# Attention's outputs as eight 64-row products a tile, and k and v in tiles of 256 rows

## The chip, the cores and the metric

The kernel runs on one core of one Trainium2 chip. The metric is the device time of one execution in microseconds. A profile of one execution stands beside three timed ones. TensorE is called PE here (PEld is its weight loads), VectorE DVE, ScalarE ACT, GpSimd POOL and SyncE SP, as in the profile.

## The reference, cut to what matters

Three parts follow each other. Linear attention over 4 batches, 8 heads, 576 positions and heads of 64 is normalised head by head; its 2304 rows of 512 go through a mixture of 8 experts, one expert a row, and then through a dense feed-forward block:

```python
kv = np.einsum('bhsd,bhse->bhde', k, v)
out = np.einsum('bhsd,bhde->bhse', q, kv)
rms = np.sqrt(np.mean(out * out, axis=-1, keepdims=True) + 1e-06)
x = (out / rms * g_norm)
...
logits = x @ w_gate
expert_idx = np.argmax(logits, axis=1)
h = np.maximum(np.einsum('ecd,edf->ecf', disp, w1), 0.0)
y = np.einsum('ecf,efd->ecd', h, w2)
...
h = x @ w_in
g = np.where(h > 0.0, h, alpha * (np.exp(np.minimum(h, 0.0)) - 1.0))
return (g @ w_out)
```

`disp` holds each expert's rows in their order of arrival, up to a capacity.

## The kernel before, in words

**Attention** (lines 107 to 397) has its order written out by hand: inside it the instructions of each engine run as the program lists them. k and v come as [2304, 512], 18 chunks of 128 rows, q transposed as `qT` [4, 128, 2304]: partition = two heads of 64 features, four such pairs. `load_kv` (line 127) and `load_q` (line 132) issue all transfers on SP's queue, in the order of lines 267 to 289; the outputs' stores to `x_dram` go to the same queue behind them. The pool `ld` holds ten chunks of each.

Chunk by chunk `kv_product` (line 149) sums k'v of each head, 64 x 64, for one batch in PSUM (`pk`): head h of a pair goes to the column half h of PE. A batch is four chunks and a half. `kv_out`, `kv_turn` and `kv_gate` (lines 167 to 186) take the sums out, transpose them and multiply by `gw`, the gate's weights times `g_norm`, so that `kva` holds for each pair of heads k'v beside k'v·gw. `kva` is a 128 x 144 block for each pair, with zeros where a row belongs to one head and the column to the other; POOL clears it (line 141), and `yT` as well (line 144).

`out_tile` (line 195) makes the outputs of 128 tokens: for each of four pairs one product of 128 rows (both heads' features), 128 columns (tokens) and 144 moving columns. A tile that lies over the border of two batches (tiles 4 and 13) is made in two parts of 64 tokens. From PSUM (`po`, two buffers) ACT takes the squares and a copy (`oz_all`); for the tiles in `POOL_SQ` POOL squares the copy instead. `out_sums` (DVE) sums the squares of a head. `chain` is the routing of a group of tiles, split into steps that the program deals out between the tiles; its last group needs all 18. `fill` issues products that nobody reads: they keep PE busy. Lines 297 to 397 are the hand-written order.

**Routing** (lines 403 to 494) turns the choices into `ids`, the list of rows by expert. POOL then gathers rows from `x_dram` by these lists (`gather`, line 535).

**The first window** (`first_window`, line 616) prepares the first expert's 352 rows: three gathered tiles are scaled (DVE), transposed (PE), copied as high part `xh` (ACT) and low part `xl` (DVE). `h_piece` issues the first layer's products for the expert's first two slices u = 0 and 1 as rows become ready, 12 products for each slice and each piece of rows. Then come the 64 steps of the experts (`step`, line 973), where `place` scales and transposes further gathered rows, and the dense block.

Of the kernel before, what the change touches and what calls it, by code (L numbers as in the profile page):

```python
# [20 lines left out]
P = 128  # L21
# [20 lines left out]
def block_kernel(ctx, tc, qT, k, v, g_norm, w_gate, w1, w2, w_in, w_out, out, cap, **_):  # L42
# [27 lines left out]
    ld = early.enter_context(tc.tile_pool(name="ld", bufs=10))  # L70
# [4 lines left out]

    ones = const.tile([P, P], F16, name="ones")
# [30 lines left out]
    KA = D * 2 + 2 * E  # L107
    with ExitStack() as actx:
# [18 lines left out]
        def load_kv(c):  # L127
            for t, src, n in ((kt, k, "kt"), (vt, v, "vt")):
                t[c] = ld.tile([P, C], F32, name=n)
                nc.sync.dma_start(out=t[c], in_=src[c * P:(c + 1) * P])  # L130
# [8 lines left out]
        for b in range(B):  # L139
            t = ap1.tile([P, NP, KA], F32, name=f"kva{b}")  # L140
# [4 lines left out]
        HALF = [slice(0, D), slice(D, P)]  # L145

        pk = {}
# [23 lines left out]
        def kv_turn(b):  # L171

            pt = ps_t.tile([P, NP // 2, P], F32, name="pt")
            for n in range(NP // 2):
                nc.tensor.transpose(pt[:, n], kvs[b][:, n * P:(n + 1) * P], ident)
            for h in range(2):
                nc.scalar.activation(kva[b][HALF[h], :, h * D:(h + 1) * D], pk[b][HALF[h]], AF.Copy)
            kvT[b] = ap2.tile([P, NP // 2, P], F32, name="kvT")
            nc.vector.tensor_copy(kvT[b], pt)

        def kv_gate(b):
# [3 lines left out]
            for h in range(2):  # L185
                nc.vector.tensor_copy(kva[b][HALF[h], :, P + h * E:P + (h + 1) * E], pz[HALF[h], :, :, h].rearrange("p n a e -> p (n a) e"))

# [3 lines left out]
        oz_all = ap1.tile([P, NT, NP, KA], F32, name="oz_all")  # L191
# [3 lines left out]
        def out_tile(i):  # L195
            po = ps_o.tile([P, NP, 256], F32, name="po")
# [9 lines left out]
            o = oz[:, :, 0:P]  # L206
            if i in POOL_SQ:
                nc.scalar.activation(oz, po[:, :, 0:KA], AF.Copy)
                nc.gpsimd.tensor_tensor(out=sq, in0=o, in1=o, op=ALU.mult)
            else:  # L210
                nc.scalar.activation(sq, po[:, :, 0:P], AF.Square)
                nc.scalar.activation(oz, po[:, :, 0:KA], AF.Copy)
# [13 lines left out]
        def chain(i0, G):  # L226

            def t_(shape, name):
# [16 lines left out]
                                  in0=oz_all[:, i0:i0 + G].rearrange("p g j c -> p (g j) c")[:, :, P:KA].rearrange("p k (h e) -> p k h e", h=2),  # L245
# [21 lines left out]
        for c in range(3):  # L267
            load_kv(c)
        for h in range(2):
            nc.scalar.dma_start(out=g_col[HALF[h]], in_=g_norm.rearrange("(d o) -> d o", o=1))  # L270
        for a in range(2):
            for n in range(NP // 2):
                j = 2 * n + a
                nc.scalar.dma_start(out=wg[HALF[a], n], in_=w_gate[j * P:(j + 1) * P].rearrange("(h c) e -> c h e", h=2))
# [3 lines left out]
        for c in range(3, 5):  # L278
            load_kv(c)
        load_q(0, [(0, 256), (256, S)])  # L280
        for c in range(5, 9):
            load_kv(c)
        load_q(1, [(0, 320), (320, S)])
        for c in range(9, 14):
            load_kv(c)
        load_q(2, [(0, 256), (256, S)])
        for c in range(14, 18):
            load_kv(c)
# [9 lines left out]
        fill(6)  # L298
        for c in range(5):
            chunk(0, c, (3, 3, 4, 3, 0)[c])  # L300
# [9 lines left out]
        kv_product(1, 1, 2)  # L310
        out_tile(2)
        out_sums(1)
        kv_product(1, 2, 4)
        out_sums(2)
        kv_product(1, 4, 5)
        kv_out(1)
        out_tile(3)
        kv_turn(1)
        out_sums(3)
        step(ca, 1)  # L320
        fill(2)
        kv_gate(1)
        step(ca, 1)
        fill(2)
        out_tile(4)
        step(ca, 3)
        kv_product(2, 0, 1)
        out_tile(5)
        out_sums(4)
        step(ca, 2)  # L330
        kv_product(2, 1, 3)
        out_tile(6)
        out_sums(5)
        step(ca, 2)
        kv_product(2, 3, 5)
        kv_out(2)
        out_tile(7)
        kv_turn(2)
        out_sums(6)
        step(ca, 1)  # L340
        out_tile(8)
        kv_gate(2)
        out_sums(7)
        step(ca, 2)
        kv_product(3, 0, 3)
        step(ca, 4)
        out_tile(9)
        out_sums(8)
        step(cb, 1)
        kv_product(3, 3, 5)  # L350
        kv_out(3)
        step(cb, 1)
        out_tile(10)
        kv_turn(3)
        out_sums(9)
        step(cb, 3)
        out_tile(11)
        kv_gate(3)
        out_sums(10)
        step(cb, 2)  # L360
        out_tile(12)
        out_sums(11)
        step(cc, 1)
        step(cb, 3)
        out_tile(13)
        step(cc, 1)
        out_sums(12)
        step(cb, 2)
        step(cc, 2)
        out_tile(14)  # L370
        step(cb, 1)
# [4 lines left out]
        step(cc, 3)  # L376
        out_tile(16)
        out_sums(15)
        out_tile(17)
# [169 lines left out]
    def place_scale(a):  # L549
        xg = xg_t[a]  # L550
        v = xg[:, 0:C].rearrange("p (h d) -> p h d", h=H)
        nc.vector.scalar_tensor_tensor(out=v, in0=v, scalar=used[:, a:a + 1], in1=xg[:, C:C + H].to_broadcast([P, H, D]),
                                       op0=ALU.mult, op1=ALU.mult)
# [50 lines left out]
    def h_piece(u, w, low):  # L604
# [5 lines left out]
        for j in range(NP):  # L610
# [5 lines left out]
    def first_window(fill):  # L616
# [9 lines left out]
        def turn(a):  # L626
# [697 lines left out]
```

## Time and profile before

| | us |
|---|---|
| median of three timed executions (691.22 to 691.6) | 691.48 |
| the profiled execution | 690.72 |
| its span, first to last instruction | 688.9 |
| PE busy in the span | 674.6 (98%) |
| DVE, ACT, POOL busy | 478.8, 389.0, 101.8 |

The profiled execution has 1.8 us around its span and lies 0.76 us under the median. Times of rows are counted from the start of the span. The timeline merges neighbouring instructions of a line into one row, with the number of them behind an x; a product of 32-bit numbers counts as two instructions.

### The profile page before, as it was taken

Reading aid. Unit: us, or ns where it says so; the run is one execution under the profiler, and the core shown is the slowest. Engines: PE = TensorE matmul, PEld = TensorE weight load, DVE = VectorE, ACT = ScalarE, POOL = GpSimd, SP = SyncE. Lnnn points to the kernel's source line nnn. Section 1 sums busy time; section 2 is a strip of 40 time slices with the busy share of each in tenths; the row PEclk is TensorE's granted clock in tenths of the full one; section 3 lists DMA queues with packets and bytes.
Section 4 is the critical chain, followed back from the end, with each engine's and each line's share of the span. In section 5 each row is a group of like instructions: output and inputs, shape, how many; then the busy total and the mean of one; then the engine's idle time right before and its main releaser. Section 6 shows DMA issues by size and latency. Waiting matters only on the chain.

```text
span 688.9 us, 12042 instructions
## 1 busy us (share of the span) xinstructions
PE 674.6 (98%) x4282; PEld 630.3 (91%) x4282; DVE 478.8 (70%) x915; ACT 389.0 (56%) x821; POOL 101.8 (15%) x118
## 2 busy tenths in 40 slices
PE   8999899999999999999999999999999999999996
PEld 8888899999999999999999998888899999898995
DVE  5479476777777878978765457768767687765542
ACT  1474266555555666758766567555655657554450
POOL 7112483000001212005400000000000000002213
PEclk9999899999999999999999999999999999999999
DMA  8997774646556778945643819475374937357412
GB/s 276 394 321 198 233 218 155 206 131 217 173 185 186 234 256 273 289 147 189 227 152 117 356 47 368 152 289 204 148 283 160 361 105 298 111 210 279 178 48 91
DMA packets 67101, 145.82 MB, mean 212 GB/s; under 512 B 9312, under 2 KB 29280, under 8 KB 67040
## 3 DMA queue, kind: packets, MB, share of 16 engines
q1 hardware_dynamic: 63424, 135.44, 56.3%
q0 software_dynamic: 2880, 9.59, 4.0%
q8 instruction: 34, 0.56, 0.3%
q14 instruction: 27, 0.22, 0.1%
q10 hardware_dynamic: 736, 0.02, 0.1%
HBM read 118.92 MB, written 26.10 MB: 211 GB/s over the span
## 4 chain that ended last, share of the span: by engine, by line
PE 64%; issue 3%; POOL 1%; POOLq 0%
PE pa L1133 11%; PE acc L1174 6%; PE acc L1175 6%; PE acc L1173 6%; PE pd L1133 5%; PE ph L677 4%; PE ph L678 4%; PE ph L679 4%; PE pe L1133 3%; PE acc L1087 2%; PE acc L1088 2%; PE acc L1086 2%; PE acc L679 2%; PE acc L677 2%; PE acc L678 2%
## 5 line engine op out<-in xcount | busy, mean ns | idle before, releaser
L1133 PE MATMUL pa<-right,ab 128*128 128x384 f32 x432 | 84.5, 336 | 0.0
L1133 PEld LDWEIGHTS pa<-right,ab 128*128 128x128 f32 x432 | 76.2, 188 | 2.1 <-ACT u L1230 0.5
L677 PE MATMUL acc<-hh,w2h 128*128 128x288 f32 (+6 forms) x256 | 77.3, 302 | 0.0
L678 PE MATMUL acc<-hh,w2l 128*128 128x288 f32 (+6 forms) x256 | 76.9, 300 | 0.0
L679 PE MATMUL acc<-hl,w2h 128*128 128x288 f32 (+6 forms) x256 | 76.9, 300 | 0.0
L677 PE MATMUL ph<-xh,w1h 128*128 128x288 f32 (+6 forms) x248 | 75.0, 302 | 0.3 <-PEq L868 0.3
L678 PE MATMUL ph<-xh,w1l 128*128 128x288 f32 (+6 forms) x248 | 74.6, 301 | 0.0
L679 PE MATMUL ph<-xl,w1h 128*128 128x288 f32 (+6 forms) x248 | 74.4, 300 | 0.0
L1175 PE MATMUL acc<-w2h,gx 128*128 128x512 f32 x180 | 70.3, 390 | 0.0
L1174 PE MATMUL acc<-w2l,gx 128*128 128x512 f32 x180 | 70.2, 390 | 0.0
L1173 PE MATMUL acc<-w2h,gx 128*128 128x512 f32 x180 | 70.0, 389 | 0.0
L1181 POOL DMA_INDIRECT out<-part,ids x18 | 17.6, 977 | 324.3 <-DVE part L1178 314.7
L697 ACT ACTIVATE hh<-ph 128x288 fp32r<-128x288 f32 (+6 forms) x64 | 26.9, 421 | 67.5 <-PE ph L679 63.8
L1178 DVE TENSOR_TENSOR part<-part,acc 128x512 f32<-128x512 f32 x54 | 36.4, 684 | 37.2 <-PE acc L1175 37.2
L525 DVE TENSOR_TENSOR w2l<-a,w2h 128x512 fp32r<-128x512 f32 x64 | 50.8, 794 | 9.2 <-ACT w2h L522 9.2
L698 DVE SCALAR_TENSOR_TENSOR hl<-ph,hh 128x288 fp32r<-128x288 f32 (+6 forms) x64 | 30.0, 469 | 31.9 <-ACT hh L697 31.4
L677 PEld LDWEIGHTS acc<-hh,w2h 128*128 128x128 f32 x256 | 48.2, 188 | 0.0
L678 PEld LDWEIGHTS acc<-hh,w2l 128*128 128x128 f32 x256 | 48.2, 188 | 0.0
L679 PEld LDWEIGHTS acc<-hl,w2h 128*128 128x128 f32 x256 | 48.2, 188 | 0.0
L677 PEld LDWEIGHTS ph<-xh,w1h 128*128 128x128 f32 x248 | 46.7, 188 | 0.5 <-ACTq L868 0.5
L678 PEld LDWEIGHTS ph<-xh,w1l 128*128 128x128 f32 x248 | 46.7, 188 | 0.1
L679 PEld LDWEIGHTS ph<-xl,w1h 128*128 128x128 f32 x248 | 46.6, 188 | 0.0
(228 smaller groups left out, 1643.3 us busy)
## 6 DMA issues: line engine op xcount, KB each, us to landing
right<-y_dram SPq DMA_DIRECT2D x63, 768.0 KB, 8.1
a<-w SPq DMA_DIRECT2D x128, 256.0 KB, 3.1
w<-w_in SPq DMA_DIRECT2D x16, 512.0 KB, 4.8
w<-w_out SPq DMA_DIRECT2D x16, 512.0 KB, 5.1
kt<-k SPq DMA_DIRECT2D x18, 256.0 KB, 7.2
vt<-v SPq DMA_DIRECT2D x18, 256.0 KB, 6.0
x_dram<-oz_all SPq DMA_DIRECT2D x18, 256.0 KB, 5.4
y_dram<-yh SPq DMA_DIRECT2D x9, 384.0 KB, 3.7
```

The costliest lines, as they stand in the source:

```text
L525: return engine.tensor_tensor(out=dst[1], in0=src, in1=dst[0].bitcast(F32), op=ALU.subtract)
L677: nc.tensor.matmul(out, lhsT=ah, rhs=bh, start=start, stop=False)
L678: nc.tensor.matmul(out, lhsT=al, rhs=bh, start=False, stop=False)
L679: nc.tensor.matmul(out, lhsT=ah, rhs=bl, start=False, stop=stop)
L697: nc.scalar.activation(hh[:, :W], ph[:, :W], AF.Relu)
L698: nc.vector.scalar_tensor_tensor(out=hl[:, :W], in0=ph[:, :W], scalar=0.0, in1=hh[:, :W].bitcast(F32), op0=ALU.max, op1=ALU.subtract)
L1133: nc.tensor.matmul(ps[:, :BT], lhsT=x[:, cs], rhs=b[:, y, k], start=(start and k == 0 and n == 0), stop=(k == KH - 1 and n == 2), skip_gro ...
L1173: nc.tensor.matmul(acc, lhsT=gh[:, ts], rhs=w2h, start=(s == 0 and c == 0), stop=False)
L1174: nc.tensor.matmul(acc, lhsT=gh[:, ts], rhs=w2l, start=False, stop=False)
L1175: nc.tensor.matmul(acc, lhsT=gl[:, ts], rhs=w2h, start=False, stop=(s == 1 and c == 1))
L1178: nc.vector.tensor_tensor(out=part[:, i], in0=part[:, i], in1=acc, op=ALU.add)
L1181: put = nc.gpsimd.indirect_dma_start(out=out, out_offset=bass.IndirectOffsetOnAxis(ap=ids[:, i:i + 1], axis=0), in_=part[:, i], in_offset= ...
```

## The change

- `out_tile` issues for each pair of heads two products, one for each head: 64 rows (the row halves of PE), 128 tokens, 72 moving columns (64 outputs and 8 of the gate). `po` has one PSUM bank for each row half. `kva` needs no zeros, and the places of the gate's columns move.
- k and v are loaded 256 rows at a time, two rows to a partition, so that a partition's piece is 4 KB; the chunk of 128 rows at the border of two batches stays alone. q of batches 0 and 1 comes in one transfer each, and the last piece of batch 2's q behind the last k and v.
- `g_norm` and `w_gate` are loaded from POOL's queue instead of ACT's; `yT` is cleared by ACT, not POOL.
- The hand-written order of attention is another one; it has fewer `fill`s.
- The first window's first tile is handled in two halves; the 224 further rows of slices 0 and 1 are one piece for both (slice 0 had two of 128 and 96), and one `place` moves ahead of step 0. In step 5 two of the `place`s move into the middle of a series of products.

```diff
-    ld = early.enter_context(tc.tile_pool(name="ld", bufs=10))
+    ld = early.enter_context(tc.tile_pool(name="ld", bufs=4))
...
+    for h in range(2):
+        nc.gpsimd.dma_start(out=g_col[HALF[h]], in_=g_norm.rearrange("(d o) -> d o", o=1))
...
-    KA = D * 2 + 2 * E
+    KA = D + E
...
+            for t, src, name in ((kt, k, "kt"), (vt, v, "vt")):
+                g = ld.tile([P, m, C], F32, name=f"{name}{m}", bufs=4 if m == 2 else 2)
+                nc.sync.dma_start(out=g, in_=src[r:r + m * P].rearrange("(p m) c -> p m c", m=m))
...
-            nc.gpsimd.memset(t, 0.0)
-            kva.append(t)
-        for j in range(NP):
-            nc.gpsimd.memset(yT[:, j], 0.0)
...
+        def clear(y):
+            nc.scalar.activation(y, zero.to_broadcast([P, y.shape[1]]), AF.Copy)
...
-            po = ps_o.tile([P, NP, 256], F32, name="po")
+            po = ps_o.tile([P, 2, 512], F32, name="po")
...
-                    nc.tensor.matmul(po[lo:hi, j, 0:KA], lhsT=q_sb[bb][:, j, ss:ss + hi - lo], rhs=kva[bb][:, j],
-                                     start=True, stop=True)
+                    for h in range(2):
+                        nc.tensor.matmul(po[lo:hi, h, j * KA:(j + 1) * KA], lhsT=q_sb[bb][HALF[h], j, ss:ss + hi - lo],
+                                         rhs=kva[bb][HALF[h], j], start=True, stop=True)
...
-            chunk(0, c, (3, 3, 4, 3, 0)[c])
+            chunk(0, c, (2, 1, 2, 1, 0)[c])
...
-        place_scale(0)
-        turn(0)
-        fill(4)
...
+        place_scale(0, 2)
+        turn(0, 2, lambda: fill(1))
+        for js in (low_half, high_half):
+            for u in range(2):
+                h_piece(u, ws[0], False, js)
...
-        for w in ws[1:]:
-            h_piece(0, w, False)
-            h_piece(0, w, True)
-        rest = slice(P, W)
-        h_piece(1, rest, False)
-        h_piece(1, rest, True)
-        placed["s"] = placed["t"] = n
+        for u in range(2):
+            h_piece(u, rest, False)
+            h_piece(u, rest, True)
+            if u == 0:
+                placed["s"] = placed["t"] = n
+                place(n + 1, 0)
...
-    QUOTA = (2, 2, 2, 2, 2, 2, 3, 0)
+    QUOTA = (1, 2, 2, 2, 2, 2, 3, 0)
```

SP's queue at the start of the program, before (kt and vt are tiles of k and v, q of qT; a bracket names what the issue waits for, DMAHW being the landing of an earlier transfer that used the same one of eight counters):

```order
L130 DMA kt<-k 128x512
L130 DMA vt<-v 128x512
L130 DMA kt<-k 128x512
L130 DMA vt<-v 128x512
L130 DMA kt<-k 128x512 [waits DMAHW0_49]
L130 DMA vt<-v 128x512 [waits DMAHW3_49]
```

The same place after the change:

```order
L143 DMA kt_152<-k 128x1024
L143 DMA vt_154<-v 128x1024
L143 DMA kt_156<-k 128x1024
L143 DMA vt_158<-v 128x1024
L143 DMA kt_166<-k 128x512
L143 DMA vt_168<-v 128x512
L151 DMA q_170<-qT 128x4x576
L143 DMA kt_172<-k 128x1024
L143 DMA vt_174<-v 128x1024 [waits DMAHW0_49]
```

Before, the fifth issue already waits for a landing (six small transfers of ACT's queue hold counters too). Now eight transfers, 3.5 MB, are issued ahead of the first wait, and each k or v transfer is as large as two were.

PE from tile 9 (the first of batch 2 alone) to tile 11, before (pk are k and v's sums, pt and pz the steps to `kva`, po the outputs):

```order
L202 MATMUL po<-kva_142,q_222 128x144 [waits DVE_49,DMAHW6_49,Activation_49,Pool_49]
L202 MATMUL po<-kva_142,q_222 128x144 x3
L162 MATMUL pk<-vt,kt 64x64 [waits DMAHW5_49,DMAHW4_49]
L162 MATMUL pk<-vt,kt 64x64 x7
L162 MATMUL pk<-vt,kt 64x64 [waits DMAHW7_49,DMAHW6_49]
L162 MATMUL pk<-vt,kt 64x64 x7
L202 MATMUL po<-kva_142,q_222 128x144 [waits PE_49,Activation_49]
L202 MATMUL po<-kva_142,q_222 128x144 x3
L175 MATMUL pt<-ident,kvs 128x128 [waits DVE_49]
```

And after the change:

```order
L217 MATMUL po<-kva_146,q_194 128x72 [waits DMAHW2_49,DVE_49,Activation_49]
L217 MATMUL po<-kva_146,q_194 128x72 [waits DVE_49,Activation_49]
L217 MATMUL po<-kva_146,q_194 128x72 x14
L176 MATMUL pk<-vt_198,kt_196 64x64 [waits DMAHW4_49,DMAHW3_49]
L176 MATMUL pk<-vt_198,kt_196 64x64 x15
L176 MATMUL pk<-vt_202,kt_200 64x64 [waits DMAHW6_49,DMAHW5_49]
L176 MATMUL pk<-vt_202,kt_200 64x64 x15
L189 MATMUL pt<-ident,kvs 128x128 [waits DVE_49]
L189 MATMUL pt<-ident,kvs 128x128
L217 MATMUL po<-kva_146,q_194 128x72 [waits DMAHW7_49,Activation_49]
L217 MATMUL po<-kva_146,q_194 128x72 x7
```

Tiles 9 and 10 now stand in a row, sixteen products for the two, and the last four chunks of k and v behind them in two blocks; tile 11 comes after the transposition.

## Rows read from the trace of the kernel before

**Rows 1.** The page: the span, and busy time of each engine.

```profile
span 688.9 us, 12042 instructions
PE 674.6 (98%) x4282; PEld 630.3 (91%) x4282; DVE 478.8 (70%) x915; ACT 389.0 (56%) x821; POOL 101.8 (15%) x118
```

**Rows 2.** Windows of 5 us: PE, PEld, DVE, ACT, POOL busy, PE clock, DMA share, GB/s.

```profile
0.00:5.00 5.00, 3.44 (x16) 3.45 (x16) 0.47 (x4) 1.28 (x1) 4.33 (x26) 1.00 0.51 125
5.00:10.00 5.00, 5.00 (x56) 4.35 (x57) 2.64 (x1) 0.00 (x0) 5.00 (x4) 1.00 0.96 299
...
75.00:80.00 5.00, 2.12 (x14) 1.79 (x13) 1.29 (x3) 2.31 (x4) 2.66 (x3) 0.88 0.95 339
80.00:85.00 5.00, 5.00 (x25) 5.00 (x25) 3.00 (x6) 0.46 (x1) 0.00 (x0) 0.50 0.49 191
85.00:90.00 5.00, 4.66 (x33) 4.27 (x32) 1.81 (x2) 3.34 (x7) 3.18 (x3) 0.94 0.31 79
```

**Rows 3.** Timeline of PE, start to tile 2: start us, us, engine, line, operation, out<-in.

```profile
1.55 2.93 PE L123 MATMUL idle<-ident 128*128 128x128 f32 x12 [1.55 <-POOL ident masks.py:199]
5.27 1.12 PE L162 MATMUL pk<-vt,kt 128*64 128x64 f32 x16
...
13.99 0.97 PE L162 MATMUL pk<-vt,kt 64*64 64x64 f32 x32
...
16.22 0.63 PE L184 MATMUL pz<-gw,kvT 128*128 128x32 f32 x4
16.69 0.69 PE L123 MATMUL idle<-ident 128*128 128x128 f32 x4
17.61 2.20 PE L202 MATMUL po<-kva,q 128*128 128x144 f32 x16 [0.23 <-DVE kva L186]
19.74 0.69 PE L162 MATMUL pk<-vt,kt 128*64 128x64 f32 x16
```

**Rows 4.** Timeline of SP's queue, the fifth and the sixth transfer.

```profile
3.46 0.33 SPq L130 DMA_DIRECT2D kt<-k  x1
6.33 0.33 SPq L130 DMA_DIRECT2D vt<-v  x1
```

**Rows 5.** Timelines of DVE and POOL before the first output tile, POOL's first gather.

```profile
7.36 7.32 DVE L276 TENSOR_SCALAR gw<-wg,g_col 64x32 f32<-64x32 f32 x2 [5.90 <-DMA wg<-w_gate]
14.79 0.42 DVE L169 COPY kvs<-pk 128x256 f32<-128x256 f32 x1
...
5.21 9.16 POOL L144 MEMSET yT<- 128x2688 f32 x4
...
65.45 1.33 POOL L546 DMA_INDIRECT xg<-x_dram,ids  x1 [5.55 <-DMA a<-w]
```

**Rows 6.** Timeline of PE in attention: around batch 1's sums, and around tile 9.

```profile
26.16 1.20 PE L202 MATMUL po<-kva,q 128*64 128x144 f32 x8
27.62 0.80 PE L202 MATMUL po<-kva,q 128*64 128x144 f32 x5 [0.27 <-DMA kt<-k]
...
38.28 1.25 PE L202 MATMUL po<-kva,q 128*128 128x144 f32 x8
39.46 1.25 PE L162 MATMUL pk<-vt,kt 128*64 128x64 f32 x32
```

**Rows 7.** Timeline of ACT, the last tiles of attention.

```profile
49.30 0.60 ACT L211 ACTIVATE sq<-po 128x512 f32<-128x512 f32 x1
49.78 0.66 ACT L212 ACTIVATE oz_all<-po 128x576 f32<-128x576 f32 x1
...
52.27 0.65 ACT L212 ACTIVATE oz_all<-po 128x576 f32<-128x576 f32 x1
```

**Rows 8.** Timeline of PE, then of ACT, in the first window.

```profile
74.53 0.64 PE L613 MATMUL ph<-xl,w1h 128*128 128x128 f32 x4
77.86 0.33 PE L613 MATMUL ph<-xh,w1h 128*128 128x128 f32 x1 [2.68 <-issue]
...
77.12 0.69 ACT L631 ACTIVATE xh<-pt,g_col 128x512 fp32r<-128x512 f32 x1 [5.13 <-remote]
```

More of the change, by code (lines that the diff above doesn't have):

```diff
@@ L74, in block_kernel @@
     nc.vector.memset(gw, 0.0)
+    HALF = [slice(0, D), slice(D, P)]
+    for h in range(2):
+        nc.gpsimd.dma_start(out=g_col[HALF[h]], in_=g_norm.rearrange("(d o) -> d o", o=1))
+    for a in range(2):
+        for n in range(NP // 2):
+            j = 2 * n + a
+            nc.gpsimd.dma_start(out=wg[HALF[a], n], in_=w_gate[j * P:(j + 1) * P].rearrange("(h c) e -> c h e", h=2))
     ones = const.tile([P, P], F16, name="ones")
@@ L125, in block_kernel, with load_kv @@
         kt, vt, q_sb = {}, {}, {}
[L127 to L130, printed above, removed]
+        def load_kv(n):
+            half, n = divmod(n, 5)
+            rows = (0, 256, 512, 640, 896, 1152)
+            m = (rows[n + 1] - rows[n]) // P
+            c = half * 9 + rows[n] // P
+            r = half * 2 * S + rows[n]
+            for t, src, name in ((kt, k, "kt"), (vt, v, "vt")):
+                g = ld.tile([P, m, C], F32, name=f"{name}{m}", bufs=4 if m == 2 else 2)
+                nc.sync.dma_start(out=g, in_=src[r:r + m * P].rearrange("(p m) c -> p m c", m=m))
+                for i in range(m):
+                    t[c + i] = g[:, i]
         def load_q(b, pieces):
@@ L265, in step @@
                 next(c)
[L267 to L274, printed above, removed]
+        for n in range(2):
+            load_kv(n)
         for a in range(2):
@@ L277, in block_kernel @@
                                     scalar1=g_col[HALF[a]], scalar2=None, op0=ALU.mult)
[L278 to L288, printed above, removed]
+        for j in range(NP):
+            clear(yT[:, j])
+        load_kv(2)
+        load_q(0, [(0, S)])
+        for n in range(3, 5):
+            load_kv(n)
+        load_q(1, [(0, S)])
+        for n in range(5, 8):
+            load_kv(n)
+        load_q(2, [(0, 256)])
+        for n in range(8, 10):
+            load_kv(n)
+        load_q(2, [(256, S)])
         load_q(3, [(0, 192), (192, 448), (448, S)])
@@ L609, in h_piece @@
             ph_early[u] = ps_h.tile([P, C], F32, name="ph")
-        for j in range(NP):
+        for j in js:
             c = slice(j * P, (j + 1) * P)
@@ L624, in first_window, with turn @@
         pts = []
[L626 removed]
+        def turn(a, pieces=1, between=None):
             xg = xg_t.pop(a)
[L628 to L631 removed]
+            m = NP // pieces
+            pts.append([])
+            for i in range(0, NP, m):
+                pt = ps_a.tile([P, m, P], F32, name="pt", tag="acc")
+                for j in range(m):
+                    nc.tensor.transpose(pt[:, j], xg[:, (i + j) * P:(i + j + 1) * P], ident)
+                nc.scalar.activation(xh[:, i:i + m, ws[a]], pt[:, :, :ws[a].stop - ws[a].start], AF.Copy, scale=g_col)
+                if between and i == 0:
+                    between()
+                pts[a].append((slice(i, i + m), pt))
             gather()
[L633 removed]
         def low(a):
[L636 to L637 removed]
+            for js, pt in pts[a]:
+                nc.vector.scalar_tensor_tensor(out=xl[:, js, ws[a]], in0=pt[:, :, :ws[a].stop - ws[a].start], scalar=g_col,
+                                               in1=xh[:, js, ws[a]].bitcast(F32), op0=ALU.mult, op1=ALU.subtract)
         def rows(a):
[L640 to L644 removed]
+            for js, pt in pts[a]:
+                nc.scalar.activation(xT[:, js, a * P:(a + 1) * P], pt, AF.Copy, scale=g_col)
+        low_half, high_half = range(NP // 2), range(NP // 2, NP)
+        rest = slice(P, W)
+        place_scale(0, 2)
[3 more added lines that the diff above has]
+                h_piece(u, ws[0], False, js)
         rows(0)
[L646 removed]
         for a in range(1, n):
@@ L983, in step, with one @@
             next(early_sums)
+        def one():
+            place(min(need[1], placed["t"] + 1), 0)
+        mid = one if u == 5 else None
         if u < NU:
-            expert_h(u)
+            expert_h(u, mid)
         q = QUOTA[u] if u < NF else 2 if more else 0
@@ L989, in step @@
         if u:
-            expert_y(u - 1)
+            expert_y(u - 1, mid)
         if q > 1:
```

122 lines of the change are left out of this document (59 added, 63 removed).

## The prediction

> **What bounds the kernel now.** I read the page first. PE is busy for 98% of the span [rows 1], and the chain that ended last is PE's, so a change pays where it makes PE's steady work behind the first window begin earlier; what PE does from there is the same in both kernels. The question is how much the part ahead of it shortens. [...] The timelines then show three stretches.
>
> Until 17.61 us PE works without a pause on fills and on the five chunks of batch 0; the first output tile follows when `kva` is there [rows 3]. From 17.61 to the last tile PE is the engine that is nearly always at work: a block of two whole tiles takes 19.74 - 17.61 = 2.13 us, a single one between k and v products 39.46 - 38.28 = 1.18 us [rows 3, 6]. With x for a tile and s for the change to another kind of product, 2x + s = 2.13 and x + s = 1.18, so x = 0.95 and s = 0.23. ACT takes about 1.0 us a tile (the squares 0.48 from start to start, the copy about 0.5) and ends shortly behind PE, at 52.9 us [rows 7]. Then the routing runs down to the first gather at 65.45 [rows 5], and the first window begins. There PE has nothing from 75.17 (74.53 + 0.64) to 77.86, since ACT's copy of the second tile comes at 77.12 after a wait whose releaser the profile calls remote, which is to say that it does not show it [rows 8]; half the clock follows.
>
> **The change part by part.**
>
> *Start of the program.* Before, SP issues its sixth transfer only at 6.33, 2.9 us behind the fifth [rows 4], and 125 and then 299 GB/s are moved in the first two windows [rows 2]. Afterwards 3.5 MB are issued ahead of the first wait. But the first products need 1.05 MB where 0.52 MB were enough: at the rates of rows 2 these are there at 6.4 us, so the first products start at some 6.6 instead of 5.27, 1.3 us later. All five chunks, 2.6 MB, would be there at 11.7 even at these rates, ahead of their need. From there seven fills fewer stand between the chunks: two instructions each, 1.6 us at the 0.115 an instruction that four gate products take, 16.22 to 16.69 [rows 3]. And chunk 0's products no longer fall into the slow start (1.12 us against 0.69 for the same sixteen [rows 3]): 0.6 with its fills. Sum: 1.3 - 1.6 - 0.6 = **-0.9 us**. Bounds: if only the fills counted -2.2; if the first megabyte is 2 us later than I think +1.1. The two fills more at the top stand in the wait for the first megabyte.
>
> POOL's six transfers, `ident` standing behind the first of them: the nearest price is a gather's issue, 1.33 us [rows 5], so PE's fills start up to 1.3 us later, hidden in the same wait. The gate's weights are then issued by 1 + 6 x 1.33 = 9 us; in the kernel before `gw` is made until 14.68, just ahead of the copy at 14.79 that it precedes on DVE [rows 5], so there are 5 us for the landing. ACT's clearing of `yT`: 512 columns take 0.48 to 0.60 [rows 7], so 2688 at most 3.2 and four 12.6 us, from 2.1 to 14.7 at the latest; by the smaller figure they end at 12.1. ACT's next work, the copy for `kva`, is due at about 14.4. POOL loses 9.16 us of clearing [rows 5] for which nobody waits. All of this at nothing; without its cover it costs some tenths.
>
> *The sixteen whole tiles.* Each has sixteen instructions where it had eight, with 72 moving columns instead of 144. What can bound them: the moving columns, half as many, or the weights, 128 columns for each instruction. The four gate products have 128 weight columns and only 32 moving ones, and still start 0.115 us apart [rows 3]. Whether the two row halves work side by side is shown in one place: the thirty-two instructions of 64 rows at 13.99 take 0.97, sixteen of 128 rows 0.69 [rows 3]; the second sixteen, which stand in the other row half, cost 0.28 more and not 0.6. So I take pairs side by side: eight pairs of 0.11 make 0.88 a tile instead of 0.95. Sixteen tiles: **-1.1 us**. Not half the time, because the weights now bound. Bounds: side by side with no weight bound 0.5 a tile (-7); one behind the other 16 x 0.115 = 1.84 (+14).
>
> *Tiles 4 and 13*, in two parts of 64 tokens. Before, a part costs what a tile does: 1.20 for eight instructions [rows 6], so the tile 1.9. Afterwards a part has 64 weight columns and 72 moving ones, the form of k and v's products, sixteen in 0.5 (0.69 less the last one's tail); the tile 1.0. Two tiles: **-1.9 us**.
>
> *Changes of form.* Output tiles no longer have the form of the transpositions and the gate products between them: for three batches, in and out of each of two blocks, 12 more changes at s = 0.23, 2.8 us at most, 0 at least. About half stand where PE waits for DVE anyway: **+1.4 us**. [...]
>
> *Order and stores.* From batch 1's last sums to the second part of tile 4, at 27.62 [rows 6], the wait for `kva` stays as long as batch 0's; a tile moves from inside it to ahead of it. I put that at 0. SP's stores stand behind all loads as before, in 512-byte pieces as before, and the routing behind them is the same.
>
> Attention: -0.9 - 1.1 - 1.9 + 1.4 = **-2.5 us**. ACT with 1.0 a tile can follow.
>
> *First window.* Slice 0's two pieces of 128 and 96 columns become one of 224: 12 products fewer. With 128 weight columns they cost 0.115 at the full clock, 0.20 in the half-clock window (25 in 5 us [rows 2]), and it is there that they stand: **-2.4 us**, 1.4 at least. The halves of the first tile let PE begin some 0.8 us earlier, but the end of the window hangs on the second and the third tile, so I count nothing. The `place` that moves ahead of step 0 and those of step 5 are the same work.
>
> Sum: -2.5 - 2.4 = -4.9 us. 690.72 - 4.9 = 685.8; the median lies 0.76 above the profiled execution, so **686.6 us**.
>
> **The rivals.**
>
> *The stop does not come back.* PE's gap and the half clock behind it are the largest loss ahead of the steady work: 2.7 us of standing [rows 8], and 1.2 + 5 + 0.6 = 6.8 us at half speed (0.88, 0.50, 0.94 of three windows [rows 2]), which cost 3.4. The cause is not shown. For its return: as many gathers and weight loads meet there as before. Against: PE, ACT and DVE now come there in another order. Without it the first window gains 2.7 + 3.4 + 12 x 0.115 = 7.5, with attention 10.0: 680.7 for the profiled execution, **681.5 us**.
>
> [...]
>
> *The row halves do not work side by side* with 128 weight columns. A tile then costs 1.84 and, since PE is what attention goes by, sixteen tiles 14.2 us more instead of 1.1 less: -0.9 + 14.2 - 1.9 + 1.4 - 2.4 = +10.4, **701.9 us**, slower. It decides from 1.2 us a tile on (16 x 0.25 = 4 eat the rest). Against it: the 0.28 us of rows 3, though with 64 weight columns.
>
> *What PE gains is waited for elsewhere* (the first megabyte late, ACT's strided reads of PSUM dearer than 1.0 us a tile, the stores): attention gains nothing, the stop comes back, and the first window's gain is all: 0 to -2, about **690.5 us**.
>
> **How the numbers follow.** Forecast 0.42, no stop 0.32, every change paid 0.09, waited for elsewhere 0.09, row halves one by one 0.08. About 0.2%, 1.4 us, is what a measurement can tell from no change. Below 690.1 lie the first three: faster 0.83. Of the fourth nearly all is within 0.2%: same 0.09. Slower 0.08. The range takes in the forecast, the rival without a stop with 2 us for the unknown costs of the start, and the paid changes: 679.5 to 690.5; some 0.17 are outside.
>
> **What would show it.** The first output tile at about 16.7 us. A whole output tile at 0.9 to 1.1 us on PE, a straddling one at 1.0. The last group's `chain` starting some 2.5 us before 53. The gap of PE ahead of the third tile's products and a window with a clock of 0.5, or neither. Twelve fewer products in the first window. I am wrong if a tile takes over 1.2 us, if the first products start after 8 us, or if ACT ends attention more than 2 us behind PE.

## The result: 0.6% slower, and the profile after

The changed kernel took 695.89 us (median of seven executions, 691.88 to 702.84) where the kernel before took 691.48 on the same chip: a ratio of 1.0062, interval 1.0036 to 1.0089. The forecast was 686.6 and the range ended at 690.5, so it failed in direction too. The executions of before lie within 3.7 us of each other, those of the change within 11. (Executions over 1.5% above the fastest of their kernel stand outside the ratios: one of the change's seven, one of e15's, three of e8's four.)

The profiled execution of the change took 700.79 us, 10.07 more than that of before. It is one of the longer ones, and this is where its time stands:

| us | before | changed | difference |
|---|---|---|---|
| first output tile on PE | 17.61 | 16.18 | -1.43 |
| last output tile ends on PE | 51.74 | 59.22 | +7.48 |
| `ids` written | 64.97 | 72.47 | +7.50 |
| `ids` to the first product of `expert_y` | 22.29 | 22.87 | +0.58 |
| from there to the end of the span | 601.64 | 603.26 | +1.62 |
| outside the span | 1.82 | 2.19 | +0.37 |

Between the first and the last output tile 7.48 + 1.43 = 8.9 us are lost, nearly all of the 10.07. The page of the profile, answering to [rows 1]:

```profile
span 698.6 us, 12263 instructions
PE 679.8 (97%) x4406; PEld 635.4 (91%) x4406; DVE 473.2 (68%) x918; ACT 399.4 (57%) x827; POOL 94.7 (14%) x116
```

The windows of 5 us, with the columns of [rows 2]:

```profile
20.00:25.00 5.00, 3.46 (x64) 2.97 (x64) 2.90 (x6) 2.90 (x7) 1.28 (x2) 1.00 1.04 412
25.00:30.00 5.00, 5.00 (x82) 4.61 (x82) 2.92 (x11) 1.79 (x3) 1.04 (x1) 0.63 1.05 407
30.00:35.00 5.00, 5.00 (x62) 4.75 (x61) 1.61 (x4) 1.14 (x2) 0.00 (x0) 0.50 1.03 408
...
45.00:50.00 5.00, 4.47 (x71) 4.16 (x70) 3.46 (x9) 1.36 (x3) 0.83 (x1) 0.50 1.13 250
50.00:55.00 5.00, 4.66 (x82) 4.07 (x81) 2.93 (x10) 3.60 (x10) 0.00 (x0) 0.98 0.24 67
...
80.00:85.00 5.00, 4.19 (x21) 4.19 (x21) 1.54 (x3) 1.68 (x4) 2.84 (x3) 0.59 0.91 302
85.00:90.00 5.00, 4.33 (x21) 3.93 (x20) 1.77 (x3) 2.43 (x4) 1.89 (x2) 0.50 0.87 319
```

PE is busy for 3.46 of 5 us from 20 on, and behind that its clock is 0.50 from 26.3 (0.63 of the window from 25) to 50: a second stretch at half the clock, in the middle of attention, where the kernel before had 1.00 throughout. The busy share hides it (97%), for an engine at half its clock counts as busy (5.00 of 5 us at 0.50 in the window from 30). The timeline of PE there (start, duration, engine, line, operation, out<-in; in brackets the idle time ahead and who ended it):

```profile
16.18 2.11 PE L217 MATMUL po<-kva,q 64*128 64x72 f32 x32
...
19.30 2.01 PE L217 MATMUL po<-kva,q 64*128 64x72 f32 x32
21.23 1.15 PE L176 MATMUL pk<-vt,kt 128*64 128x64 f32 x32
22.91 0.44 PE L189 MATMUL pt<-ident,kvs 128*128 128x128 f32 x2 [0.53 <-DVE kvs L183]
24.36 0.63 PE L198 MATMUL pz<-gw,kvT 128*128 128x32 f32 x4 [1.01 <-DVE kvT L193]
24.92 3.19 PE L217 MATMUL po<-kva,q 64*64 64x72 f32 x48
28.04 1.97 PE L176 MATMUL pk<-vt,kt 128*64 128x64 f32 x32
29.94 1.99 PE L217 MATMUL po<-kva,q 64*128 64x72 f32 x16
```

While batch 1's `kva` is made, PE waits 0.53 and 1.01 us, where in the kernel before tile 3 and four `fill`s stood ahead of the product at 26.16 [rows 6]. A little later, at 29.94, a tile takes 1.99 us; at 19.30 two took 2.01. So the question for the runs: do the waits bring the half clock, or the new products, or both?

### The profile page after: what moved, and what is told of

It is laid out like the page before. It is cut to its first block, busy times and chain, and to the rows that moved or that the text cites. A ratio compares the mean times of both kernels' runs of the same rounds, so it can differ in the third digit from the quotient of the medians.

```text
span 698.6 us, 12263 instructions
## 1 busy us (share of the span) xinstructions
PE 679.8 (97%) x4406; PEld 635.4 (91%) x4406; DVE 473.2 (68%) x918; ACT 399.4 (57%) x827; POOL 94.7 (14%) x116
## 4 chain that ended last, share of the span: by engine, by line
PE 59%; issue 3%; DMA 2%; ACT 1%; POOL 1%; DVE 1%; POOLq 0%; ACTq 0%
PE pa L1161 10%; PE acc L1202 6%; PE acc L1203 6%; PE acc L1201 6%; PE pd L1161 5%; PE ph L697 4%; PE ph L698 4%; PE ph L699 4%; PE pe L1161 3%; PE acc L1115 2%; PE acc L1116 2%; PE acc L1114 2%; DMA y_dram<-th 2%; PE acc L699 2%; PE acc L697 1%
## 5 line engine op out<-in xcount | busy, mean ns | idle before, releaser
L720 DVE SCALAR_TENSOR_TENSOR hl<-ph,hh 128x288 fp32r<-128x288 f32 (+6 forms) x64 | 30.0, 469 | 32.3 <-ACT hh L719 31.9
```

Source lines behind the costliest of these rows:

```text
L720: nc.vector.scalar_tensor_tensor(out=hl[:, :W], in0=ph[:, :W], scalar=0.0, in1=hh[:, :W].bitcast(F32), op0=ALU.max, op1=ALU.subtract)
```

## Experiments

The runs fell on several chips. On those of e1 to e12 the kernel before took 684.8 to 685.4 us, on those of e13 to e18 691.5 to 691.8, about as in the first measurement. Each ratio is to the kernel before on the same chip, and times of whole executions on different chips are not compared. A mean clock is that of a whole execution.

**e1: fills in batch 1's wait.**

```diff
         kv_out(1)
+        fill(2)
...
         kv_turn(1)
         step(ca, 2)
+        fill(4)
         kv_gate(1)
```

> Theory (the order's missing fills): the changed kernel lets PE stand still for 1.5 of the 2.6 us in which batch 1's kva is made, and the half clock from 26.7 to 50.1 us follows from that alone. With two fills behind batch 1's last k and v products and four behind its transposition, the clock is 1.00 from there to the end of attention, the row numbers are written near 62 us instead of 72.5, and the time is about 691, near the lowest execution of the changed kernel (691.9), with a smaller spread. Rival (the form of the products): products of 64 rows and 72 columns themselves bring the half clock. Then it comes here too, and the time stays at 695 to 701.

Measured: 687.52, 1.0032 of before (1.0012 to 1.0051). The theory missed in part: the half clock at 26.3 is gone, and another comes at 37.6, behind a wait of 1.08 us ahead of tile 9. DVE's timeline shows that wait's cause: `kva`'s copy stands behind the chain steps that the order deals out between `kv_turn(2)` and `kv_gate(2)`, and one of them waits for ACT's exponential.

```profile
35.86 0.19 DVE L274 TENSOR_REDUCE sm<-ex 128x4 f32<-128x32 f32 x1 [0.87 <-ACT ex L273]
36.41 0.18 DVE L276 RECIPROCAL sm<-sm 128x4 f32<-128x4 f32 x1 [0.36 <-POOL sm L275]
36.50 0.38 DVE L200 COPY kva<-pz 64x32 f32<-64x32 f32 x2
```

**e2: batch 1's piece of the order alone, with the old products.**

```diff
+        out_tile(3)
         kv_product(1, 4, 5)
         kv_out(1)
-        out_tile(3)
...
-        fill(2)
         kv_gate(1)
         step(ca, 1)
-        fill(2)
         out_tile(4)
```

> The kernel before with only batch 1's piece of the new order: tile 3 ahead of the last chunk's products, and none of the four fills. Theory (missing fills): PE stands still for 1 to 2 us near 24 to 26 us, a half clock follows in at least some executions, and the time is 694 to 701, though the products are the old ones. Rival (the form of the products): no half clock in attention and 691.5 within 1.

Measured: 686.29, 1.0020 (1.0001 to 1.0040). PE waits 0.53 and 1.33 us for the same two copies, the second longer than in the change, and in the profiled execution the clock stays at 1.00. PE's timeline:

```profile
26.78 0.63 PE L184 MATMUL pz<-gw,kvT 128*128 128x32 f32 x4 [1.33 <-DVE kvT L179]
```

The ten executions have mean clocks of 0.994 to 0.999, those of the kernel before 0.995 to 0.999, so a short half clock in one or two of them is not excluded. This contradicts the theory in its first form: a wait alone needn't bring the half clock.

**e3: the new products alone** (`out_tile`, `kva`'s layout and what reads them; before's order and fills).

> The kernel before with only the products of 64 rows and 72 columns; its order and its fills stay. Theory (missing fills): clock 1.00 throughout attention; a whole tile takes about 1.0 us on PE as in the first two of the changed kernel, a tile over two batches 1.0 in place of 1.9; by the terms of the prediction -1.1, -1.9 and +1.4 the time is about 690. Rival (the form of the products): half a clock in attention and 695 or more.

Measured: 684.48, 0.9992 (0.9969 to 1.0015), which can't be told from no change (690 was expected of a kernel at 691.5, 1.5 us less); no half clock in attention in the profile. So the products alone don't bring it either, or seldom: one of the ten executions took 690.85 at a mean clock of 0.981. PE's timeline gives their price:

```profile
19.07 0.69 PE L162 MATMUL pk<-vt,kt 128*64 128x64 f32 x16
19.68 1.12 PE L203 MATMUL po<-kva,q 64*128 64x72 f32 x16
20.73 1.62 PE L162 MATMUL pk<-vt,kt 128*64 128x64 f32 x48
...
25.37 0.72 PE L203 MATMUL po<-kva,q 64*64 64x72 f32 x16
26.33 0.95 PE L203 MATMUL po<-kva,q 64*64 64x72 f32 x16 [0.25 <-issue]
...
49.78 1.60 PE L123 MATMUL idle<-ident 128*128 128x128 f32 x12
52.37 0.42 PE L121 MATMUL idle<-a,ident 128*128 128x48 f32 x2 [0.98 <-DVE a L241]
```

A single tile takes 20.73 - 19.68 = 1.05 us where it took 1.18, and PE is through 1.9 us earlier than before (49.85 against 51.74), 0.65 of it because the first tile already starts earlier (16.96 against 17.61). But the last group's chain starts only 1.0 us earlier (52.12 against 53.13), since DVE's sums are not done: the last row shows PE waiting 0.98 us for them.

**e4: e1 with the old first window and steps.**

> The same as the run with fills, but with the first window and the steps of the kernel before. If the new first window saves what the prediction said (12 products at the half clock), this is 2.4 us slower than the run with fills. Rival (the new window leaves PE without fills while it waits for the first rows, and so pays 13 instead of 7 us at the half clock): this is up to 3 us faster than the run with fills.

Measured: 689.59, 1.0064 (1.0041 to 1.0088), 2.1 us more than e1. Inconclusive by itself, for its profiled execution also has more of the half clock in attention than e1's: `ids` is written at 70.42 against 66.84, while `ids` to `expert_y` takes 16.15 against 15.74.

**e5: the change once more**, on a chip of the faster kind.

> The changed kernel once more, beside the next three on one chip. Theory (two waits opened by the order): a half clock of 7 us or more in attention in most executions, median 1.003 to 1.012 of the kernel before. Rival (only the chip of the first comparison does this): 0.995 to 1.000, as the terms of the prediction without the clock.

Measured: 691.12, 1.0082 (1.0055 to 1.0109). The theory came in. The half clock in attention is there again, at other times: from 39 to 42.4 and from 45.9 to 59.5. Behind batch 1's waits, the same 0.53 and 1.01 us as in the first profile, the clock stays at 1.00 this time:

```profile
25.41 0.63 PE L198 MATMUL pz<-gw,kvT 128*128 128x32 f32 x4 [1.01 <-DVE kvT L193]
...
25.00:30.00 5.00, 4.59 (x96) 4.26 (x96) 3.32 (x13) 2.14 (x5) 0.81 (x1) 1.00 1.05 406
```

So the same program and the same wait bring the half clock in one execution and not in another.

**e6: e1 with the second wait mended too** (`kv_gate(2)` ahead of `step(ca, 4)`, two fills ahead of tile 9 and two ahead of `kv_turn(3)`).

> The run with fills, and in addition batch 2's gate products and their copies ahead of the four chain steps of the first group (in the change DVE does those first, one of them waits for ACT's exponential, and PE waits 1.1 us for batch 2's kva), two fills ahead of tile 9 and two ahead of batch 3's transposition. Theory (the order's waits): clock 1.00 throughout attention, last output tile at 49 to 50 us in place of 53.6, 2 to 4 us less than the run with fills, so 683 to 685 where before is 685.4. Rival (the form of the products): a half clock in some executions still, and a median above 686.

Measured: 689.89, 1.0078 (1.0061 to 1.0095), so the theory's 683 to 685 missed. The clock now holds to 44, and a third wait has become the long one. PE stands 2.62 us for batch 3's sums, whose copy is on DVE behind a group's chain and two tiles' sums:

```profile
39.97 0.69 DVE L234 TENSOR_REDUCE sums<-sq 128x8 f32<-128x512 f32 x1 [1.19 <-POOL sq L225]
...
42.20 0.68 DVE L234 TENSOR_REDUCE sums<-sq 128x8 f32<-128x512 f32 x1
42.91 0.42 DVE L183 COPY kvs<-pk 128x256 f32<-128x256 f32 x1
```

Behind it the clock is 0.50 from 44 to 61.

**e7: the second wait mended alone.**

> The changed kernel with batch 2's gate products ahead of the chain steps and two fills ahead of tile 9, but without any fill in batch 1. Theory: of the two waits this mends the second; the half clock that follows the first (from 26.7 us) stays in part of the executions, and the time lies between the changed kernel and the run with all mended. If the first wait alone made the loss, no gain against the changed kernel; if the second alone, as fast as the run with all mended.

Measured: 694.38 in four executions from 687.99 to 697.94, 1.0157 (1.0111 to 1.0204): no gain against e5 (1.0082), so nothing shows that mending the second wait alone buys anything. In the profiled execution the half clock comes three times in attention, the first time at 26.4, behind batch 1's waits.

**e8: the two single parts of e2 and e3 together.**

> The kernel before with the new products and with batch 1's piece of the new order without fills, which are the two single parts put together. With the old products that order left PE idle for 1.9 us between 24.5 and 26.8 and the clock stayed at 1.00. Theory (idle time alone): again no half clock there, about 685. Rival (idle time together with the products of 64 rows): a half clock from 27 us on in most executions, 688 or more.

Measured: three executions of 698.63 to 701.47 and one of 684.58, so no ratio is given. In the profiled one the clock is 0.50 from 27 to 68. It fits "both together", and I don't rest the case on it.

**e9: e6 with the third wait mended too** (`kv_out(3)`, `kv_turn(3)`, tile 11 and `kv_gate(3)` ahead of the sums and chain steps).

> The run with the order mended, and in addition batch 3's sums copied out at once: in the change that copy stands on DVE behind nine steps and sums, among them the sums of tile 9 that wait for POOL's squares, and PE waits 2.6 us for it near 42 us. Theory (waits and products of 64 rows together bring the half clock): with this third wait gone the clock stays at 1.00 in attention, the last output tile ends near 49.5 us in place of 57, and the time is 682 to 684 where before is 684.8. Rival (the products of 64 rows lose the clock at any small wait): a half clock in most executions still, 686 or more.

Measured: 687.69, 1.0048 (1.0032 to 1.0065): the theory missed. The clock holds to 47.6, and there my own order made a fourth wait: with eight chain steps dealt out ahead of tile 12, ACT's exponential stands in front of that tile's squares and waits 2.20 us for DVE, and PE 2.13 for ACT. Then half the clock to 58.

**e10: the change with the old products.**

```diff
-    KA = D + E
+    KA = D * 2 + 2 * E
...
-            kva.append(ap1.tile([P, NP, KA], F32, name=f"kva{b}"))
+            t = ap1.tile([P, NP, KA], F32, name=f"kva{b}")
+            nc.gpsimd.memset(t, 0.0)
+            kva.append(t)
...
+                    nc.tensor.matmul(po[lo:hi, j, 0:KA], lhsT=q_sb[bb][:, j, ss:ss + hi - lo], rhs=kva[bb][:, j],
+                                     start=True, stop=True)
```

> The changed kernel with the products of before (128 rows, 144 columns, kva with its zeros) and everything else of the change, its three waits too. Theory (both are needed): no half clock in attention, or seldom; 684.5 to 687. Rival (the waits alone bring it): a half clock as in the changed kernel, 689 or more.

Measured: 688.45, 1.0065 (1.0048 to 1.0082): slower than the theory's 684.5 to 687, and without a half clock in attention in the profiled execution. Against e5 this is the clearest pair. Two windows of e10:

```profile
35.00:40.00 5.00, 3.09 (x36) 2.71 (x35) 2.98 (x10) 2.68 (x8) 0.76 (x3) 1.00 1.11 342
40.00:45.00 5.00, 2.75 (x71) 2.47 (x69) 3.61 (x10) 1.58 (x3) 1.04 (x1) 1.00 1.20 287
```

The same windows of e5, the change itself, and a later one:

```profile
35.00:40.00 5.00, 3.58 (x48) 3.23 (x45) 2.64 (x11) 2.45 (x7) 0.80 (x3) 0.90 1.11 346
40.00:45.00 5.00, 3.87 (x74) 3.56 (x74) 3.85 (x10) 1.90 (x4) 0.76 (x1) 0.76 1.20 288
...
50.00:55.00 5.00, 5.00 (x50) 4.89 (x48) 3.29 (x9) 3.50 (x7) 0.00 (x0) 0.50 0.73 196
```

With the old products PE stands still more (3.09 and 2.75 of 5 us busy) and keeps its clock; with the new ones it stands less and loses it. The executions that were not profiled make the pair less sharp: mean clocks are 0.997, 0.996, 0.993 and 0.994 in e10 and 0.984, 0.985, 0.993 and 0.987 in e5, so some half clock may lie in e10's too. And e10 shows what the order costs without any half clock: its last tile ends at 54.54 (51.74 before), its chain starts at 55.93 (53.13), 2.8 us later, although its first tile starts 0.8 us earlier (16.80). From the first to the end of the last tile it takes 37.7 us, the kernel before 34.1: 3.6 us are the order's. PE's timeline of e10 has the waits:

```profile
25.20 0.63 PE L200 MATMUL pz<-gw,kvT 128*128 128x32 f32 x4 [0.91 <-DVE kvT L195]
...
38.54 2.20 PE L218 MATMUL po<-kva,q 128*128 128x144 f32 x16 [1.56 <-POOL rr L275]
...
45.08 0.44 PE L191 MATMUL pt<-ident,kvs 128*128 128x128 f32 x2 [2.32 <-DVE kvs L185]
```

**e11: e3 with the new first window and steps.**

> The kernel before with the new products and the new first window with its steps; attention's order, loads and fills are those of before. With the products alone the time was 684.5 where before was 685.4. If the window is worth the 2.4 us of the prediction: 682. Theory: on a chip where PE does not stand still in the first window 12 products at the full clock are worth 1.4 at most, and the traces show 0.4 to 1.0 us between the list of rows and the first product of the second layer: 683.4 to 684.1.

Measured: 684.25, 0.9993 (0.9980 to 1.0006): with the half clock absent from the window (PE's longest wait there is 0.67 us, the mean clock 0.997), the new one can't be told from the old (e3 had 0.9992).

**e12: e9 with the old first window and steps.**

> The run with all three waits mended, but with the first window and the steps of before. The prediction's term (12 products at the half clock): 2.4 us slower than with the new window. Theory (12 products at the full clock, part of them beside waits): 0.4 to 1.4 slower. Rival (the new window is worth nothing here): the same.

Measured: 689.30, 1.0072 (1.0055 to 1.0089), 1.6 us more than e9, a little over the theory's 0.4 to 1.4 and under the prediction's 2.4; `ids` to `expert_y` took 16.41 us where e9 took 15.37.

**e13: the change with attention's order and fills of before** (from `ca, cb, cc, cd` to the last `out_sums` only; loads, products and window stay).

> The changed kernel with attention's order and fills of before: its loads, products, first window and steps stay. Theory (the order is the cause): clock 1.00 in attention, no wait of PE over 1 us there, 683 to 685 where before is 684.8, that is 0.997 to 1.001. Rival (the loads, the products or the window share in the loss): 1.003 or more.

**e14: the same with the start's fills of the change.**

```diff
-        fill(6)
+        fill(8)
         for c in range(5):
-            chunk(0, c, (3, 3, 4, 3, 0)[c])
+            chunk(0, c, (2, 1, 2, 1, 0)[c])
```

> As the run with the old order, but the start's fills are those of the change (eight at the top, then 2, 1, 2, 1 behind the chunks, in place of six and 3, 3, 4, 3). The prediction's term for the start: first output tile some 0.9 us earlier than in the kernel before (17.6), against the run with the old order up to 1.6. If attention is bound by PE, the time falls by as much; if DVE's sums and chain set its end, by less than 0.5.

Measured: e13 691.09, 0.9991 (0.9968 to 1.0015); e14 689.91, 0.9965 (0.9946 to 0.9985). Both keep the clock at 1.00 in attention, and among the new products PE waits no longer than 0.28 us there. A window of e14, and the start of the last group's chain on DVE, in the kernel before and in e14:

```profile
25.00:30.00 5.00, 4.75 (x106) 4.26 (x102) 2.89 (x10) 2.25 (x5) 1.01 (x1) 1.00 1.06 409
...
53.13 0.19 DVE L237 TENSOR_SCALAR a<-sums 128x48 f32<-128x48 f32 x1
...
50.77 0.19 DVE L255 TENSOR_SCALAR a<-sums 128x48 f32<-128x48 f32 x1
```

So the order, with the fills that go with it, was the loss: undone, the change isn't slower, and with its start it is faster. Both ran on chips where the kernel before takes 691.5 to 691.8; on the others only e3 and e11 have the old order, and they are as fast as the kernel before. The start's fills alone bring the first tile from 17.70 to 16.23 and `ids` from 63.99 to 62.61; the medians differ by 1.2, with intervals that overlap.

**e15: e9 with the fourth wait mended** (the exponential behind tile 13).

> The run with all three waits mended, with ACT's exponential of the second group moved from ahead of tile 12's squares to behind those of tile 13. Theory (waits and new products together): no wait of PE over 1 us is left, the clock stays at 1.00 in attention, the last tile ends at 49 to 51 us, 683 to 685. Rival (the new products lose the clock anyhow): half clock again, 687 or more.

Measured: 694.26, 1.0042 (1.0013 to 1.0071): the theory missed, and the rival's half clock and time came. ACT now has the next group's logarithm ahead of tile 13's squares and waits 2.41 us for DVE, PE 2.80 for ACT. And in the profiled execution the clock falls at 36, where PE's only recent wait was 0.34:

```profile
35.79 0.93 PE L198 MATMUL pz<-gw,kvT 128*128 128x32 f32 x4 [0.34 <-DVE kvT L193]
36.54 1.20 PE L130 MATMUL idle<-ident 128*128 128x128 f32 x4
37.67 3.69 PE L217 MATMUL po<-kva,q 64*128 64x72 f32 x32
```

e6 and e9 had the same wait at the same place and kept the clock there. How little is enough stays open.

**e16: e14 with the old first window and steps. e17: e14 once more. e18: e14 with eight fills more behind the first tile's transpositions.**

> The run with the old order and the change's start, but with the first window and the steps of before. The prediction's term (12 products at the half clock): 2.4 us slower than with the new window where PE stops in the window, 1.4 where it does not. Theory by the traces so far: from the list of rows to the first product of the second layer the new window took 23.2 and 23.4 us with a stop (22.3 in the kernel before) and 15.4 to 15.8 without (16.4 with the old one), so about 1 us faster with a stop and 0.5 to 1 us slower without.

> The run with the old order and the change's start once more, beside the others of this call. Theory (the order alone made the change slow): 0.994 to 0.999 of the kernel before again. Rival (the first result was the chip's): 1.000 or more.

> The run with the old order and the change's start, with eight fills more behind the first tile's transpositions in the first window. Theory (PE loses its clock there while it waits for ACT's late first copy): where there is a stop, the half clock of 7 to 11 us in the window becomes shorter or goes, 1 to 3 us faster than without the fills; where there is none, up to 1.3 us slower. Rival (the fills end before the stop does): as slow or slower in both cases.

Measured: e16 693.59, 1.0023 (0.9999 to 1.0048); e17 688.35, 0.9963 (0.9946 to 0.9981); e18 692.89, 1.0025 (1.0009 to 1.0041). e17 repeats e14's gain. Against e17, e16 puts the new window's worth at 5.2 us on this chip, more than any of the expectations, and e18's fills cost 4.5, as its rival said: PE's wait there is 3.87 us with them, 1.79 (e17) and 4.57 (e14) without. PE's timeline at the first product behind the first tile, in e17:

```profile
70.60 0.33 PE L629 MATMUL ph<-xh,w1h 128*128 128x128 f32 x1 [1.79 <-ACT xh L650]
```

The same product in e14:

```profile
73.77 0.47 PE L629 MATMUL ph<-xh,w1h 128*128 128x128 f32 x1 [4.57 <-ACT xh L650]
```

And in e18:

```profile
75.99 0.33 PE L629 MATMUL ph<-xh,w1h 128*128 128x128 f32 x1 [3.87 <-remote]
```

e14 and e17 are the same program: the stop takes 1.79 us in one execution and 4.57 in the other. It comes at the same piece of work and not with the same length.

## Why the prediction was wrong, step by step

**Order and stores, put at 0: the step that failed.** The prediction looked at batch 1 alone, said that "the wait for `kva` stays as long as batch 0's", and left out that batch 0's has four fills in it which the change takes from batch 1. It did not follow DVE's queue past the moved chain steps in batches 2 and 3. The order opens waits of PE of 0.5 and 1.0 us (batch 1), 1.1 to 1.6 (batch 2) and up to 2.6 (batch 3). By themselves they cost 3.6 us between the first and the last tile (e10), where 0 was put, and in every profile that has them with the new products the clock falls as well. With the old order both losses are gone (e13, e14, e17). In the profiled execution of the change the two together made +7.5 us up to `ids`: behind batch 1's waits PE ran at half its clock for 24 us, and the later waits, 0.37 and 0.53 us there, were covered by a PE that was itself late. Of the signs of being wrong one came, a tile of over 1.2 us (1.99 from 29.94 on), but by the clock and not by row halves that work one by one.

**The clock in attention was on no list.** The prediction counted fills as time in PE's way and named what hides them; it did not ask what clock PE has behind the waits that they cover. In attention the nine profiles with the new order and the new products together all show a half clock (the change, e1, e4 to e7, e9, e12, e15; e8 is left aside), and none of the ten with one of them or neither does (before, e2, e3, e10, e11, e13, e14, e16 to e18). What decides in a single case stays open: batch 1's waits kept the clock in e5, a wait of 0.34 us was enough in e15, and one of e3's executions that were not profiled has a mean clock of 0.981. Nor is it shown what brings the clock back: from 30 to 40 us of the change PE is busy for all 10 us, and the clock stays at 0.50.

**Start of the program, -0.9: right in sign and about in size.** The first products start at 6.56 (6.6 predicted), the first tile at 16.18 (16.7), and in the other profiles with the change's start at 16.2 to 17.4. Between e13 and e14 the start's fills are worth 1.4 us at `ids`.

**Whole tiles -1.1, straddling tiles -1.9, changes of form +1.4: right in sum, in part by luck.** -1.6 was predicted. From the first tile to the end of the last e13, e14 and e17 take 32.2 to 32.3 us where the kernel before takes 34.1: -1.9. With the old loads it is less, 32.9 in e3 and 33.8 in e11, where PE waits for transfers of v (0.23 to 0.33 us each), so a part of it seems to be the new loads', for which the prediction had no term behind the start. A pair among k and v's products takes 21.23 - 19.30 = 1.93 and a single tile 1.05, so x = 0.88 and s = 0.17, where 0.88 and 0.23 were assumed. The row halves do work side by side with 128 weight columns (0.88 us a tile, where 1.84 was put for one behind the other), and the rival of 701.9 us falls. A change of form comes to 0.17 us by these two times. No run shows how many of the 12 are paid, so neither the +1.4 (half of them) nor the "every change paid" of the chances and the range; what the runs show is 0.17 us for one, and the -1.9 for the three terms together. A part of 64 tokens takes 0.72 to 0.95 and not 0.5, and tile 4 takes 1.85 us in e13 (26.03 to 27.88, 0.25 of it a wait) and not 1.0; the other two terms came out better than they were put.

**Attention, -2.5.** With the old order most of it comes out: the chain starts at 50.77 (e14), 51.10 (e17), 51.64 (e16) and 51.81 (e18) against 53.13, -1.3 to -2.4. The rival "waited for elsewhere" holds for a part, the 0.98 us for DVE's sums in e3 and 0.99 in e14.

**First window, -2.4: right in sign, its size hangs on the stop.** Without the stop it is worth nothing that e11 can tell, 1.6 us in e9 against e12; with it 5.2 in e17 against e16. Single profiles with the stop don't show it: `ids` to `expert_y` takes 20.87 to 23.37 us with the new window (e17, e15, the change, e13, e14), 22.29 and 24.72 with the old one (before, e16). The half clock of the window then lasts 10.2 us in e17 and 13.6 in e16: more than the 12 products of the sum lies under it.

**The rival without a stop.** On the chip of the first measurement the stop came back (PE idle from 78.83 to 80.81), with 13.7 us of half clock behind it in place of 6.8. In none of the profiles of e1 to e12 does it come, whichever kernel ran. Its return was not the change's doing, and a chance of 0.32 for its absence had no ground in the change.

**The 1.6 us behind the window** are for 1.4 us waits for `hh` and `hl` near 294 (0.81 and 0.62 us), where in the kernel before PE is busy throughout (280 to 300). The prediction's "what PE does from there is the same in both kernels" did not hold. In e5, the change's other profile, the same waits are 1.22 and 0.62 us, a half clock of 3.4 us follows, and the stretch takes 606.71 us, 5.1 more than in the kernel before. PE's timeline and a window of e5:

```profile
285.79 0.39 PE L697 MATMUL acc<-hh,w2h 128*128 128x256 f32 x1 [1.22 <-ACT hh L719]
...
289.00:290.00 1.00, 1.00 (x7) 1.00 (x7) 1.00 (x4) 0.66 (x2) 0.00 (x0) 0.50 0.96 366
```

In e1, e6 and e9 the stretch takes 601.6 to 601.7 us again; what made the waits was not tried.

The best version found is e14, the change with attention's old order: 0.9965 and 0.9963 of before, twice.

## What to carry to other kernels

When a change deals out an in-order queue's work anew, follow every copy that another engine waits for past the steps that now stand ahead of it, on each queue; each mended wait here uncovered the next one. Fills that nobody reads also cover a wait: price their removal by the wait that then stands open, and by what may follow it at half the clock, not by their own duration. (That a fill as such holds the clock isn't shown: e2, and e5 in batch 1, kept it without.) And look at the granted clock by windows before reading a busy share: 97% busy was here an engine at half speed for 24 us in attention alone.

## What the runs showed of the hardware that I had not expected

- **In attention the clock fell behind waits with one kind of product and not with the other.** With products of 128 rows and 144 columns PE waited 1.56 and 2.32 us (e10) at 1.00; with those of 64 rows and 72 columns the clock fell behind waits of 0.34 to 2.80 us (in e15 once within the wait) and stayed at 0.50 for 7 to 24 us (the change, e1, e6, e9, e15), in which PE was at work nearly all the time. It is no rule for all products: in e5's steady work the clock fell with products of 128 rows and 256 columns, behind waits of 1.22 and 0.62 us, and with the same products it stayed at 1.00 in the change, behind 0.81 and 0.62. How short a wait is short enough was not found.
- **The stop in the first window goes with the chip.** PE's longest wait between 60 and 100 us is 1.19 to 4.57 us in the kernel before, the change and e13 to e18, and 0.98 at most in e1 to e12. Where the stop comes, the issues of SP's queue change with it: in the kernel before, e13 and e14 several lie 1.41 to 1.71 us apart and last 0.00 or 0.01 us, and in the change one gap is 2.15 us. SP's timeline in the kernel before:

```profile
72.75 0.33 SPq L585 DMA_DIRECT2D a<-w  x1
74.19 0.00 SPq L584 DMA_DIRECT2D a<-w  x1
75.60 0.01 SPq L585 DMA_DIRECT2D a<-w  x1
77.03 0.01 SPq L584 DMA_DIRECT2D a<-w  x1
```

SP's timeline in e11, on a chip without the stop, with issues 0.6 apart:

```profile
72.95 0.33 SPq L591 DMA_DIRECT2D a<-w  x1
73.62 0.33 SPq L590 DMA_DIRECT2D a<-w  x1
```

The kernel before takes 6 to 7 us less on the chips without it; on the others a few of its executions, down to 685.9 us at a mean clock of 0.999, seem to go without it as well. What makes it was not found.
